# Whole rows for twelve of the sixteen second-layer weight tiles, on one Trainium2 core

## The chip, the core and the metric

The program runs on one NeuronCore of a Trainium2 chip. Its engines are TensorE (PE: matrix products, with weight loads listed apart as PEld), VectorE (DVE), ScalarE (ACT), GpSimd (POOL) and SyncE (SP). SyncE computes nothing here: its queue issues all DMA transfers, in order, to sixteen DMA engines. The metric is the device time of one execution in microseconds, as the median of several runs.

## The reference

A Nystrom attention (8 batches of 576 tokens, 8 heads of 64) feeds a gated MLP (512 to 1536 to 512), and this a soft mixture of 8 experts with 4 slots each. The last part, which the change is in, is this:

```python
logits = x @ phi                                  # 4608 tokens x 32 slots
d = softmax(logits, over tokens); c = softmax(logits, over slots)
slot_input = (d.T @ x).reshape(8, 4, 512)
for e in range(8):
    h = np.maximum(slot_input[e] @ w1[e], 0.0)    # w1[e]: 512 x 1024
    slot_out[e] = h @ w2[e]                       # w2[e]: 1024 x 512
return c @ slot_out.reshape(32, 512)              # 4608 x 512, float32
```

## The kernel before

The batches go through attention, gated MLP and slot logits in a long pipeline that fills the first 577 us. What follows is the tail. The slot inputs are summed up and multiplied through (lines 1159 to 1202), and the 32 slots pass the experts' two layers. The weights of these, 16.8 MB each, come from memory in tiles of 1 MB, `ffn_load(t, ...)` (line 1029): tiles 0 to 15 are `w1`, in rows of 512 columns, and tiles 16 to 31 are `w2`.

A tile of `w2` holds 256 rows of the hidden dimension (two blocks `c` of 128) and 256 of the 512 output columns, for four experts; two DMAs load it, one for each block. Tiles 16 to 23 belong to the left column half (`dh = 0`), tiles 24 to 31 to the right one. There are 22 buffers (`ffn_tags`, line 1049). `pump(n)` (line 1152) issues the loads up to tile n as buffers come free: tile t takes the buffer of tile t - 22.

Both layers multiply four experts side by side: a product of 128 rows of weights writes the 32 partitions of its expert in one PSUM tile. The first layer (line 1226) runs in two halves `nh` of the hidden dimension, each closed by a ReLU into `hF` (line 1235), four transposes (line 1238) and two copies into `FT`, from which the second layer takes its left operands. Hidden blocks 0 to 3 come from the first half.

The second layer (line 1273) runs once for each column half: 64 products of 256 columns add up in PSUM, lines 1288 and 1289 make `SR` out of the sum (high and low parts, for products in the fast float format), and `outputs(dh, SR)` (line 1250) multiplies the softmax weights of all 4608 tokens with it. That takes 36 products of 128 tokens by 256 columns; two share a PSUM tile, which ScalarE or VectorE in turn copies to an output buffer `ob`, and after 2, 4, 8, 16, 24, 32 and 36 blocks of 128 tokens (`GROUPS`) SyncE is told to write the group out, in rows of 1 KB.

The softmax weights `c` of a batch have to be turned before they can be left operands. `c_split(b)` (line 1206) does this for one batch: it splits the weights into parts (lines 1212 to 1215, on ScalarE, VectorE and GpSimd), turns them with five transposes on TensorE (lines 1219 and 1223), and copies the result out of PSUM (lines 1221 and 1224). All eight batches use the same working area, so that one split follows the other. In the text a *split* is one such call. They are written after the products of each of the tiles 16 to 23, so all before the first outputs.

What is written down is not the order in which an engine runs: in this part a planner orders each engine's instructions by the written order and by its own estimate of when each is ready. SyncE's queue and the engines then run that order as it stands.

Of the kernel before, what the change touches and what calls it, by code (L numbers as in the profile page):

```python
# [8 lines left out]
F32 = mybir.dt.float32  # L9
F32R = mybir.dt.float32r  # L10
AF = mybir.ActivationFunctionType
ALU = mybir.AluOpType
# [6 lines left out]
B, H, S, D = 8, 8, 576, 64  # L19
# [36 lines left out]
def nystrom_softmoe_kernel(  # L56
# [15 lines left out]
    pe, act, dve, pool, sp = nc.tensor, nc.scalar, nc.vector, nc.gpsimd, nc.sync  # L72
# [21 lines left out]
    psp = ctx.enter_context(tc.tile_pool(name="psp", bufs=1, space=PSUM))  # L94
# [9 lines left out]
    hi_sign, lo_mask = cst[:, 416:417], cst[:, 417:418]  # L104
# [15 lines left out]
    def big(tag, name):  # L120
        return bigp.tile([128, 2048], F32, tag=tag, name=name)
# [4 lines left out]
    def part(i, k):  # L126
        return HB[i][:, 2048 * k:2048 * k + 2048]
# [853 lines left out]

    TANH = [{(3, 1), (4, 0), (4, 1)}, {(1, 1), (2, 0), (2, 1)}]
    GROUPS = [2, 2, 4, 8, 8, 8, 4]


    pool.memset(one, 1.0)
# [6 lines left out]
    for x in S_["loads"]:  # L993
        k, n = x[0], x[1:]
# [31 lines left out]
    ffn_t = {}  # L1026

    def ffn_load(t, *bufs):
        if t < 16:
            nh, g, c = t // 8, (t // 4) % 2, t % 4  # L1030
            n = 4 // len(bufs)
            bt = []
            for i, buf in enumerate(bufs):
                src = w1[4 * g + n * i:4 * g + n * i + n, 128 * c:128 * c + 128, 512 * nh:512 * nh + 512]
                x = buf.rearrange("p (e f) -> p e f", e=n)
                sp.dma_start(x, src.rearrange("e p f -> p e f"))
                bt += [x[:, e, :] for e in range(n)]
        else:
            buf, = bufs
            dh, g, r = (t - 16) // 8, (t // 4) % 2, t % 4  # L1040
            bt = buf.rearrange("p (c e d) -> p c e d", c=2, e=4)
            for c in range(2):
                f0 = 256 * r + 128 * c
                sp.dma_start(bt[:, c], w2[4 * g:4 * g + 4, f0:f0 + 128, 256 * dh:256 * dh + 256].rearrange("e p d -> p e d"))
        ffn_t[t] = bt

    last = nb - 1
# [1 line left out]
    ffn_tags = ([f"fw{i}" for i in range(NW)] + ["00", "01", "02", "w3", "w4", "w5"] + [f"fx{i}" for i in range(NX)]  # L1049
                + ["12", "11", "w0", "w1", "w2"])  # L1050
# [4 lines left out]
    def wbuf(tag, name):  # L1055
        if tag[:2] in ("fw", "fx"):
            return (fwp if tag[1] == "w" else fxp)[0].tile([128, 2048], F32, tag=tag, name=name)
        return big(tag, name) if tag[0] == "w" else part(int(tag[0]), int(tag[1]))

    def ffn_prefetch(t):  # L1060
        ffn_load(t, wbuf(ffn_tags[t % len(ffn_tags)], f"ffn{t}"))
# [37 lines left out]
    for b in range(nb):  # L1099
        if b == 1:  # L1100
            middle = n_ins()
        for j in range(NJ):
            p = prev
# [48 lines left out]
    def pump(n):  # L1152
        while nxt[0] < min(n, 32):
            ffn_prefetch(nxt[0])
            nxt[0] += 1

    NT = len(ffn_tags)
    pump(NT - 3)
    m = psp.tile([128, 512], F32, tag="x", name="m_s", bufs=3)
# [8 lines left out]
    hF, SH = misc[:, 0:512], misc[:, 512:768].bitcast(F32R)  # L1168
# [11 lines left out]
    FT = part(1, 0).rearrange("p (g i x) -> p g i x", g=2, i=8)  # L1180
    pool.memset(FT, 0.0)
    m = psp.tile([128, 512], F32, tag="x", name="m_si", bufs=3)
# [6 lines left out]
    m = psp.tile([128, 512], F32, tag="x", name="m_sit", bufs=3)  # L1189
# [16 lines left out]
    def c_split(b):  # L1206

        if b % 2 == 0:
            cT[b // 2] = wbuf(ffn_tags[11 + b // 2], f"cT{b // 2}").bitcast(F32R)[:, 0:2 * S]
        c3 = misc[:, 768:1408].bitcast(F32R).rearrange("p (k j a x) -> p k j a x", k=5, j=4, a=4)  # L1210
        ch = CN[:, b].rearrange("p k (j x) -> p k j x", j=4)
        act.copy(c3[:, :, :, 0, :], ch)
        dve.tensor_copy(c3[:, :, :, 1, :], ch)
        dve.tensor_tensor(out=c3[:, :, :, 2, :], in0=ch, in1=c3[:, :, :, 0, :], op=ALU.subtract)
        pool.memset(c3[:, :, :, 3, :].bitcast(F32), 0.0)
        m = psp.tile([128, 512], F32, tag="x", name="m_ct", bufs=3)
        c3f = c3.bitcast(F32).rearrange("p k j a x -> p k (j a x)")
        for k in range(4):
            pe.transpose(m[:, 128 * k:128 * k + 128], c3f[:, k, :], ident)  # L1219
        o = cT[b // 2][:, S * (b % 2):S * (b % 2) + S]  # L1220
        act.copy(o[:, 0:512], m)
        m = psp.tile([128, 512], F32, tag="l", name="m_ct2")
        pe.transpose(m[:, 0:64], c3f[0:64, 4, :], ident[0:64, 0:64])  # L1223
        dve.tensor_copy(o[:, 512:576], m[:, 0:64])

    for nh in range(2):
        m = psp.tile([128, 512], F32, tag="pg", name="m_f1", bufs=2)
        for g in range(2):
            for c in range(4):
                t = 8 * nh + 4 * g + c  # L1230
                for e in range(4):
                    pe.matmul(m[32 * e:32 * e + 32, :], ZP[c][:, 4 * g + e, :], ffn_t[t][e],  # L1232
                              start=(g, c) == (0, 0), stop=(g, c) == (1, 3))
                pump(t + 1 + NT)
        act.activation(hF, m, AF.Relu)
        m = psp.tile([128, 512], F32, tag="x", name="m_ft", bufs=3)
# [10 lines left out]
    free = ffn_tags[15:21] + ffn_tags[10:11] + ffn_tags[0:2]  # L1247
    nob = [0]

    def outputs(dh, SR):  # L1250
        k0, nk = 0, nb * S // 128
        for n in GROUPS:
            n = min(n, nk - k0)
            if n <= 0:
                break
            ob = wbuf(free[nob[0] % len(free)], f"ob{nob[0]}").rearrange("p (k d) -> p k d", k=8)
            nob[0] += 1
            for k in range(k0, k0 + n, 2):
                w = min(2, k0 + n - k)
                m = psp.tile([128, 512], F32, tag=("pg", "pv")[k // 2 % 2], name="m_o", bufs=2)  # L1260
                for i in range(w):
                    t, o = divmod(128 * (k + i), 2 * S)
                    pe.matmul(m[:, 256 * i:256 * i + 256], cT[t][:, o:o + 128], SR, start=i == 0, stop=i == w - 1)  # L1263
                o = ob[:, k - k0:k - k0 + w, :].rearrange("p k d -> p (k d)")
                if k // 2 % 2:
                    act.copy(o, m[:, 0:256 * w])  # L1266
                else:
                    dve.tensor_copy(o, m[:, 0:256 * w])  # L1268
            sp.dma_start(out[128 * k0:128 * (k0 + n), 256 * dh:256 * dh + 256].rearrange("(k p) d -> p k d", p=128),
                         ob[:, 0:n, :])  # L1270
            k0 += n

    for dh in range(2):
        m = psp.tile([128, 512], F32, tag="pg", name="m_f2", bufs=2)
        for g in range(2):
            for r in range(4):
                t = 16 + 8 * dh + 4 * g + r
                for c in range(2):
                    for e in range(4):
                        pe.matmul(m[32 * e:32 * e + 32, 0:256], FT[:, g, 2 * r + c, 32 * e:32 * e + 32],  # L1280
                                  ffn_t[t][:, c, e, :], start=(g, r, c) == (0, 0, 0), stop=(g, r, c) == (1, 3, 1))
                pump(t + 1 + NT)
                if dh == 0 and 4 * g + r < nb:
                    c_split(4 * g + r)
        if dh == 0:
            SR2 = wbuf(ffn_tags[21], "SR")
        SR = SR2[:, 256 * dh:256 * dh + 256].bitcast(F32R)
        act.activation(SH, m[:, 0:256], AF.Copy, scale=hi_sign)  # L1288
        dve.scalar_tensor_tensor(out=SR, in0=m[:, 0:256], scalar=lo_mask, in1=SH, op0=ALU.mult, op1=ALU.add)  # L1289
        outputs(dh, SR)  # L1290


# [54 lines left out]
```

## Time and profile before

| | us |
|---|---|
| median of 3 runs | 662.58 (660.92 to 663.43) |
| the profiled execution | 661.27 |
| its span, first to last instruction | 659.2 |

The profile shows one execution. Times in it count from the span's start. An instruction group has its line, the engine, the tile written and the tiles read, and the busy time; TensorE's instructions overlap, so what one costs is read from the chain, where each piece counts only what it added. A DMA share near 1 means that all sixteen DMA engines are busy; it can exceed 1 by a little. A DMA that SyncE issues stands in its timeline with the time that issuing it took.

### The profile page before, as it was taken

How to read it: one execution, taken by the hardware profiler on the slowest of the kernel's cores; microseconds unless marked ns; L12 is line 12 of the kernel's file. 1: busy time of each engine (PE TensorE's matmuls, PEld its weight loads, DVE VectorE, ACT ScalarE, POOL GpSimd, SP SyncE). 2: the span in 40 equal slices, each digit the busy share in tenths (PEclk: the TensorE clock that was granted, in tenths of full speed). 3: DMA queues.
4: the chain of work that ended last, by engine and by line, in shares of the span. 5: the costliest groups of instructions: out<-in, count | busy, mean ns of one | idle time of the engine just before them, and what ended most of it. 6: DMA issues, size and time to landing. Idle time of an engine off the chain costs nothing. (4 is left out here: it accounts for less than half of the span.)

```text
span 659.2 us, 18308 instructions
## 1 busy us (share of the span) xinstructions
PE 620.1 (94%) x7591; PEld 464.7 (70%) x7591; DVE 471.8 (72%) x1154; ACT 300.1 (46%) x764; POOL 72.6 (11%) x81
## 2 busy tenths in 40 slices
PE   5699899999999999999999999999999999989991
PEld 2576677777777877777777877787778877743561
DVE  4999989889578687859785978597857555550441
ACT  2566985465338223823382338233822442320441
POOL 0410012013011101210120013001300000010000
PEclk9699999999999999999999999999999999999996
DMA  7889774453022222222222231222130596599999
GB/s 283 280 300 340 297 269 146 123 180 95 2 74 85 76 73 77 85 75 73 91 69 75 73 108 55 73 73 74 24 122 2 146 387 223 205 327 348 348 371 330
DMA packets 63298, 106.47 MB, mean 162 GB/s; under 512 B 4976, under 2 KB 33008, under 8 KB 61680
## 3 DMA queue, kind: packets, MB, share of 16 engines
q1 hardware_dynamic: 63216, 105.32, 47.6%
q8 instruction: 59, 0.97, 0.6%
q14 instruction: 23, 0.19, 0.1%
HBM read 91.24 MB, written 12.58 MB: 158 GB/s over the span
## 5 line engine op out<-in xcount | busy, mean ns | idle before, releaser
L313 ACT ACTIVATE u<-pg 128x288 f32<-128x288 f32 x174 | 71.9, 413 | 161.3 <-PE pg L946 152.7
L975 DVE TENSOR_TENSOR hT<-u,pv 128x288 f32<-128x288 f32 x174 | 78.0, 449 | 44.2 <-PE pv L946 37.9
L946 PE MATMUL pg<-EH,GH 128*128 128x288 f32 x384 | 93.9, 325 | 2.3 <-ACT u L313 1.4
L780 DVE TENSOR_TENSOR GL<-g,GH 128x512 fp32r<-128x512 f32 (+1 forms) x122 | 65.5, 568 | 33.6 <-ACT GH L766 33.6
L946 PE MATMUL pg<-EH,GL 128*128 128x288 f32 x384 | 86.1, 299 | 1.4 <-DVE GL L780 1.0
L946 PE MATMUL pv<-EH,GH 128*128 128x288 f32 x384 | 84.3, 299 | 0.3 <-ACT GH L766 0.3
L946 PE MATMUL pg<-EL,GH 128*128 128x288 f32 x384 | 82.7, 296 | 0.0
L946 PE MATMUL pv<-EL,GH 128*128 128x288 f32 x384 | 82.3, 295 | 0.0
L946 PE MATMUL pv<-EH,GL 128*128 128x288 f32 x384 | 82.1, 294 | 0.0
L766 ACT CAST GH<-g 128x512 fp32r<-128x512 f32 (+1 forms) x122 | 54.2, 496 | 55.1 <-PE g L749 55.0
L946 PEld LDWEIGHTS pg<-EH,GH 128*128 128x128 f32 x384 | 59.6, 189 | 25.2 <-issue 18.0
L800 DVE STREAM_TRANSPOSE HB<-hT 128x576 f32<-128x576 f32 x96 | 74.3, 774 | 1.8
L946 PEld LDWEIGHTS pg<-EH,GL 128*128 128x128 f32 x384 | 62.3, 188 | 5.1 <-DVE GL L780 4.2
L946 PEld LDWEIGHTS pv<-EH,GH 128*128 128x128 f32 x384 | 61.6, 188 | 2.4 <-issue 1.8
L946 PEld LDWEIGHTS pg<-EL,GH 128*128 128x128 f32 x384 | 61.6, 188 | 0.7 <-issue 0.7
L946 PEld LDWEIGHTS pv<-EL,GH 128*128 128x128 f32 x384 | 61.5, 188 | 0.7 <-issue 0.7
L946 PEld LDWEIGHTS pv<-EH,GL 128*128 128x128 f32 x384 | 61.6, 188 | 0.5 <-issue 0.5
L749 PE MATMUL g<-w,WB 64*32 64x512 f32 (+1 forms) x976 | 56.5, 510 | 0.4 <-ACT WB L536 0.4
L795 PE MATMUL l<-hT,P_sb 128*32 128x160 f32 (+1 forms) x768 | 44.7, 298 | 1.5 <-DVE hT L975 1.1
L795 PEld LDWEIGHTS l<-hT,P_sb 128*32 128x32 f32 x768 | 15.1, 108 | 40.4 <-DVE hT L975 15.8
L914 PE MATMUL m_d<-HB,HB 32*32 32x384 f32 x864 | 35.2, 491 | 0.0
L914 PE MATMUL m_d<-HB,DN 32*32 32x384 f32 x288 | 35.1, 491 | 0.0
(248 smaller groups left out, 940.4 us busy)
## 6 DMA issues: line engine op xcount, KB each, us to landing
k<-in_kT_dram SPq DMA_DIRECT2D x52, 288.0 KB, 3.8
ffn<-in_w_dram SPq DMA_DIRECT2D x13, 1024.0 KB, 8.8
ffn<-in_w_dram SPq DMA_DIRECT2D x24, 512.0 KB, 8.8
HB<-in_w_cat_dram SPq DMA_DIRECT2D x8, 1024.0 KB, 8.4
v<-in_v_dram SPq DMA_DIRECT2D x8, 1024.0 KB, 5.9
q<-in_qT_dram SPq DMA_DIRECT2D x28, 288.0 KB, 3.0
HB<-in_w_out_dram SPq DMA_DIRECT2D x12, 512.0 KB, 6.2
wr<-in_w_cat_dram SPq DMA_DIRECT2D x4, 1024.0 KB, 9.1
```

What stands on the lines that cost most here:

```text
L313: i = act.activation(*a, **kw)
L749: pe.matmul(gs[r][32 * hp:32 * hp + 32, 0:256 * n].rearrange("p (u f) -> p u f", u=n), WB[b % 2][64 * r:64 * r + 64, hp, :], w[64 * r:64 * ...
L766: act.copy(H_, g)
L780: dve.tensor_tensor(out=GL, in0=g, in1=GH, op=ALU.subtract)
L795: pe.matmul(L[32 * c:32 * c + 32, 0:32 * k], P_sb[:, j, :], main[:, 0:k, c, :], start=j == 0, stop=j == NJ - 1)
L800: dve.transpose(HB[b % 2][:, S * j:S * j + S].rearrange("p (t r) -> p t r", r=32), hT[:, 0:S].rearrange("p (t r) -> p t r", r=32))
L914: pe.matmul(ms[a][32 * g:32 * g + 32, 0:384].rearrange("p (j f) -> p j f", j=NJ), d_of(a, g, k), hb[32 * a:32 * a + 32, :, 4 * k + g, :], ...
L946: pe.matmul(ps[:, 0:HALF], G_t[b, j, q, sel_][h], e[:, q, ts_], start=n == 0, stop=n == 5)
L975: dve.tensor_tensor(out=o, in0=u, in1=pv[:, 0:HALF], op=ALU.mult)
```

## The change

Tiles 16 to 27 of `w2` become whole: a tile holds one block of 128 hidden rows and all 512 columns of four experts, and one DMA loads it. The last four hidden blocks of the second group of experts stay in column halves, as tiles 28 and 29 (left) and 30 and 31 (right). The twelve whole tiles are multiplied first, in products of 512 columns, into one PSUM tile that ScalarE copies to `hF`. Then for each column half the two remaining tiles are multiplied, VectorE adds the copied sum, and `SR` and the outputs follow as before. Splits 0 to 3 are written after the first four whole tiles; splits 4 to 7 now stand in `outputs`, each ahead of the first group of blocks that needs it (4 and 5 ahead of the fifth group, 6 and 7 ahead of the sixth). The PSUM tiles of the second layer move from the tag `pg` to the tag `x`.

```diff
+    WHOLE = 12
...
+        elif t < 16 + WHOLE:
+            buf, = bufs
+            g, fc = divmod(t - 16, 8)
+            bt = buf.rearrange("p (e d) -> p e d", e=4)
+            sp.dma_start(bt, w2[4 * g:4 * g + 4, 128 * fc:128 * fc + 128, :].rearrange("e p d -> p e d"))
         else:
             buf, = bufs
-            dh, g, r = (t - 16) // 8, (t // 4) % 2, t % 4
+            dh, r = divmod(t - 16 - WHOLE, (16 - WHOLE) // 2)
             bt = buf.rearrange("p (c e d) -> p c e d", c=2, e=4)
             for c in range(2):
-                f0 = 256 * r + 128 * c
-                sp.dma_start(bt[:, c], w2[4 * g:4 * g + 4, f0:f0 + 128, 256 * dh:256 * dh + 256].rearrange("e p d -> p e d"))
+                f0 = 128 * (WHOLE - 8 + 2 * r + c)
+                sp.dma_start(bt[:, c], w2[4:8, f0:f0 + 128, 256 * dh:256 * dh + 256].rearrange("e p d -> p e d"))
...
+    split = set()
     def outputs(dh, SR):
...
+            for b in range((128 * (k0 + n) - 1) // S + 1):
+                if b not in split:
+                    c_split(b)
+                    split.add(b)
             ob = wbuf(free[nob[0] % len(free)], f"ob{nob[0]}").rearrange("p (k d) -> p k d", k=8)
...
+    m2 = psp.tile([128, 512], F32, tag="x", name="m_f2", bufs=3)
+    SR2 = wbuf(ffn_tags[21], "SR")
+    for i in range(WHOLE):
+        g, fc = divmod(i, 8)
+        for e in range(4):
+            pe.matmul(m2[32 * e:32 * e + 32, :], FT[:, g, fc, 32 * e:32 * e + 32], ffn_t[16 + i][:, e, :],
+                      start=i == 0, stop=i == WHOLE - 1)
+        pump(16 + i + 1 + NT)
+        if i < 4:
+            c_split(i)
+            split.add(i)
+    act.copy(hF, m2)
     for dh in range(2):
-        m = psp.tile([128, 512], F32, tag="pg", name="m_f2", bufs=2)
-        for g in range(2):
-            for r in range(4):
-                t = 16 + 8 * dh + 4 * g + r
-                for c in range(2):
-                    for e in range(4):
-                        pe.matmul(m[32 * e:32 * e + 32, 0:256], FT[:, g, 2 * r + c, 32 * e:32 * e + 32],
-                                  ffn_t[t][:, c, e, :], start=(g, r, c) == (0, 0, 0), stop=(g, r, c) == (1, 3, 1))
-                pump(t + 1 + NT)
-                if dh == 0 and 4 * g + r < nb:
-                    c_split(4 * g + r)
...
+        m3 = psp.tile([128, 512], F32, tag="x", name="m_f2", bufs=3)
+        cols = slice(256 * dh, 256 * dh + 256)
+        for r in range((16 - WHOLE) // 2):
+            t = 16 + WHOLE + (16 - WHOLE) // 2 * dh + r
+            for c in range(2):
+                fc = WHOLE - 8 + 2 * r + c
+                for e in range(4):
+                    pe.matmul(m3[32 * e:32 * e + 32, 0:256], FT[:, 1, fc, 32 * e:32 * e + 32], ffn_t[t][:, c, e, :],
+                              start=(r, c) == (0, 0), stop=fc == 7)
+        SR = SR2[:, cols].bitcast(F32R)
+        R_ = hF[:, cols]
+        dve.tensor_tensor(out=R_, in0=R_, in1=m3[:, 0:256], op=ALU.add)
+        act.activation(SH, R_, AF.Copy, scale=hi_sign)
+        dve.scalar_tensor_tensor(out=SR, in0=R_, scalar=lo_mask, in1=SH, op0=ALU.mult, op1=ALU.add)
         outputs(dh, SR)
```

## Rows read from the trace of the kernel before

**Rows 1.** The page, its second part: DMA share in 40 slices of the span.

```profile
DMA  7889774453022222222222231222130596599999
```

**Rows 2.** Stretches: busy time of each engine, granted clock, DMA share, GB/s (last).

```profile
586.00:587.00 1.00, 0.99 (x7) 0.80 (x10) 1.00 (x3) 0.00 (x0) 1.00 (x2) 1.00 0.99 242
...
600.00:610.00 10.00, 10.00 (x90) 3.11 (x82) 0.65 (x2) 1.18 (x3) 0.00 (x0) 1.00 1.09 348
...
620.00:631.00 11.00, 10.48 (x86) 7.63 (x78) 7.63 (x19) 7.71 (x16) 0.69 (x3) 1.00 1.10 348
...
632.00:644.00 12.00, 10.72 (x143) 7.09 (x136) 4.26 (x7) 3.78 (x8) 0.00 (x0) 1.00 1.09 383
...
644.00:656.00 12.00, 1.57 (x10) 1.16 (x10) 2.15 (x4) 1.58 (x3) 0.00 (x0) 0.67 1.09 386
...
656.00:657.00 1.00, 0.00 (x0) 0.00 (x0) 0.00 (x0) 0.00 (x0) 0.00 (x0) 0.50 0.66 231
```

**Rows 3.** Timeline of SyncE's queue: start, us spent issuing, line, tiles, count.

```profile
517.91 9.65 SPq L1036 DMA_DIRECT2D ffn<-in_w_dram  x6
...
585.27 3.06 SPq L1044 DMA_DIRECT2D HB<-in_w_dram  x4
...
625.25 1.25 SPq L1044 DMA_DIRECT2D HB<-in_w_dram  x1
...
626.59 2.58 SPq L1269 DMA_DIRECT2D out_dram<-ob  x2
```

**Rows 4.** The chain that ended last: start, us, engine, tile, line, count.

```profile
602.68 6.36 PE m_f L1232 x57
...
609.04 0.22 PE m_f L1280
...
610.45 0.66 PE m_ft L1238 x4
...
611.10 0.56 PE m_f L1280 x6
...
618.10 0.59 PE m_ct L1219 x4
...
620.33 0.59 PE m_ct L1219 x4
...
621.12 1.46 PE m_f L1280 x22
...
623.64 0.52 PE m_o L1263 x2
...
624.19 0.70 DVE ob L1268
...
631.21 7.09 PE m_f L1280 x128
```

**Rows 5.** Stretches again, where first-layer weights are loaded.

```profile
519.00:520.00 1.00, 1.00 (x24) 0.43 (x26) 0.67 (x2) 0.08 (x1) 0.00 (x0) 1.00 0.83 143
...
536.00:544.00 8.00, 7.78 (x87) 5.99 (x88) 3.98 (x10) 2.78 (x9) 0.00 (x0) 1.00 1.05 386
```

**Rows 6.** DMA issues by tile: count, KB each, us from issue to landing.

```profile
HB<-DN SPq DMA_DIRECT2D x72, 20.0 KB, 1.8
```

**Rows 7.** Instruction groups by shape, 575 to 660: busy us, mean ns, idle before.

```profile
L1289 DVE SCALAR_TENSOR_TENSOR SR<-m_f,cst,Sacc 128x256 fp32r<-128x256 f32 x2 | 1.0, 483 | 7.9 <-ACT Sacc L1288 7.9
```

**Rows 8.** Timeline of ScalarE and VectorE, first half of the outputs.

```profile
626.41 0.33 ACT L1212 CAST Sacc<-CN 128x160 fp32r<-128x160 f32 x1
...
626.63 1.08 ACT L1266 COPY HB<-m_o 128x512 f32<-128x512 f32 x2
...
628.14 0.59 ACT L1221 CAST cT<-m_ct 128x512 fp32r<-128x512 f32 x1 [0.43 <-PE m_ct L1219]
...
628.66 2.35 ACT L1266 COPY ob<-m_o 128x512 f32<-128x512 f32 x4
...
631.25 0.69 DVE L1268 COPY HB<-m_o 128x512 f32<-128x512 f32 x1 [0.36 <-PE m_o L1263]
```

More of the change, by code (lines that the diff above doesn't have):

```diff
@@ L1271, in outputs @@
             k0 += n
-    for dh in range(2):
-        m = psp.tile([128, 512], F32, tag="pg", name="m_f2", bufs=2)
-        for g in range(2):
-            for r in range(4):
-                t = 16 + 8 * dh + 4 * g + r
-                for c in range(2):
-                    for e in range(4):
-                        pe.matmul(m[32 * e:32 * e + 32, 0:256], FT[:, g, 2 * r + c, 32 * e:32 * e + 32],
-                                  ffn_t[t][:, c, e, :], start=(g, r, c) == (0, 0, 0), stop=(g, r, c) == (1, 3, 1))
-                pump(t + 1 + NT)
-                if dh == 0 and 4 * g + r < nb:
-                    c_split(4 * g + r)
[L1285 to L1289, printed above, removed]
+    m2 = psp.tile([128, 512], F32, tag="x", name="m_f2", bufs=3)
[10 more added lines that the diff above has]
+    act.copy(hF, m2)
+    for dh in range(2):
+        m3 = psp.tile([128, 512], F32, tag="x", name="m_f2", bufs=3)
[12 more added lines that the diff above has]
+        dve.scalar_tensor_tensor(out=SR, in0=R_, scalar=lo_mask, in1=SH, op0=ALU.mult, op1=ALU.add)
         outputs(dh, SR)
```

## The prediction

> **What bounds the kernel now.** I read the page's DMA strip first, because the change is about transfers: through the last fifth of the span the sixteen DMA engines are full [rows 1]. The table by stretches, read next, says with what. From 600 to 631 the queue carries 348 GB/s at a share of 1.09 to 1.10 (three rows, alike); from 632 to 656 it carries 383 to 386 GB/s at the same share [rows 2]. The code tells the two apart: the loads of the second layer (16.8 MB, in rows of 256 columns, 1 KB) are all issued before the first output [rows 3], and everything goes through SyncE's one queue in order. So the slower stretch is the loads, the faster one the outputs. The outputs are 4608 x 512 x 4 B = 9.44 MB, 24.4 us at 386; the full rate stops at about 656.6 (231 GB/s in the microsecond from 656), so their bytes start at about 632.1, just where the rate steps up [rows 2].
>
> The list of SyncE's issues shows why they start then. The last load is issued at 625.25, the first output right behind it at 626.59 [rows 3], though its block left PSUM at 624.89 (624.19 plus 0.70 in the chain of waits) [rows 4]. The outputs wait for the loads ahead of them. TensorE holds nothing up: its second half of products ends at 638.30 (631.21 plus 7.09) [rows 4], while the first half's outputs, 12.2 us of bytes, move until about 644. The end is therefore: end of the loads, plus 24.4 us of outputs, plus 2.6 us to the span's end at 659.2. The run took 661.27 us, 2.07 beyond its span.
>
> **What the rows of 2 KB give.** Tiles 16 to 27 become one DMA each in rows of 512 columns. Rows of 2 KB are in the trace: from 536 to 544 only first-layer weights and the output projection move, both in 2 KB rows, at 386 GB/s [rows 5]. A tile is 1.049 MB: 3.01 us at 348, 2.72 at 386, so 0.296 us less each. Tile 16 does not count: the load behind it is issued only at 585.27, when a buffer comes free [rows 3], and the rate falls to 242 GB/s in the microsecond from 586 [rows 2]; a quicker tile 16 makes that dip longer. Eleven tiles x 0.296 = 3.3 us. The loads then end at 632.1 - 3.3 = 628.8. Bounds: 0, should w2's rows run as they do now, and 3.6 with all twelve. I take 3.3, since the 2 KB rows were read from a full queue, as these will be. The other four tiles keep 1 KB rows.
>
> The Trainium skill, page "DMA: Bandwidth & Descriptors", section Specifications, gives 512 B as the smallest transfer for line rate, by which 1 KB rows are at line rate already and this change would leave the loads' end at 632.1 (the third rival below). The 348 against 386 GB/s of this trace speak against that.
>
> **What the new order costs.** So far the first half of the outputs needed half the loads; now it needs tiles 16 to 29, all but two. The hand-over from loads to outputs, covered today, has to be worked out.
>
> *Loads.* Tile 29 is in at 628.8 - 2 x 3.01 = 622.8, plus 1 to 2 us until it is seen (20 KB take 1.8 us from issue to landing [rows 6]).
>
> *TensorE.* The first layer is untouched; its last transposes start at 610.45 and take 0.66 [rows 4]. The twelve tiles have 12 x 4 products of 512 columns, two instructions each (the 64 products of a half are 128 instructions [rows 4]): 96. Today 10 instructions of the second layer run before 610 (128 less the 118 in the six pieces from 611.10 to 621.12) [rows 4]; I give one tile, 8, the same place. A 512-column instruction costs 6.36/57 = 0.112 us, a 256-column one 7.09/128 = 0.055 [rows 4], so the wider product itself gains and costs nothing. 88 x 0.112 = 9.8. Four splits stand among them, 0.79 each (620.33 to 621.12 [rows 4]): 3.2. Products cut into by splits cost more: the six pieces take 7.73 us for 118 instructions, 1.2 over 118 x 0.055, so 0.24 for each of five splits; for four, 1.0. Then tiles 28 and 29, 32 x 0.055 = 1.8. Sum: 610.45 + 0.66 + 9.8 + 3.2 + 1.0 + 1.8 = 626.9. Tile 29's products begin near 626.0, so its load is hidden by 1 to 2 us. The copy of the 512 columns to SBUF lies beside the products of tiles 28 and 29 on an idle ScalarE.
>
> *To the first output.* From the last product to the first output product it takes 623.64 - 622.58 = 1.06 now, and the first block is out of PSUM 1.25 later [rows 4]. The added sum on VectorE is 128x256 out of PSUM, 0.48 by the one of that size [rows 7], with a hand-over 0.5. 626.9 + 1.06 + 0.5 + 1.25 = 629.7 for the first issue. From an issue into an empty queue to bytes: issued at 517.91 [rows 3], and in the microsecond before 520 it moved 143 KB [rows 5], 0.4 us at full rate, so 1.7 us. The outputs' bytes start at 631.4, against 632.1 now, and 2.6 us after the loads have ended. That gap is where the gain goes: 0.7 of 3.3 us is left.
>
> *Bounds of the hand-over.* The instructions do not run in the written order: eight splits are written ahead of the first half's end, but only five stand before 621.12 in the chain, and a piece of second-layer products runs inside the first layer at 609.04 [rows 4]. If the four later splits were drawn ahead of tile 29, TensorE would be 4 x (0.79 + 0.24) = 4.1 later and the end 3.4 later than now. At the other end, if the products were never late, the outputs would follow the loads directly: 3.3 earlier than now. I take the middle because the splits go one every 2.2 us (618.10 to 620.33 [rows 4]), so that four written early take 9 of the 16 us, and those written later stand behind tile 29.
>
> *Between output blocks.* Splits 4 to 7 now stand before the fifth and sixth output DMA. Each takes 0.33 and 0.59 of ScalarE [rows 8] and three short steps of VectorE, and the evictions behind them wait. Today the ends of three splits run there as well: with them, group 4 (blocks 8 to 15) was out of PSUM at 627.71, 4.07 after 623.64, and group 5 at 629.84, two of the four copies from 628.66, 6.2 after [rows 8]. The first issue comes 1.25 after; groups 1 to 3 are 8 blocks, 2.7 us of bytes, so group 4 is needed at 4.0 and is 0.1 late; group 5 is needed at 6.8 and, with about 1 us for one split more, is ready at 7.2. I put 0.3 us of empty queue for it (0 to 2). The second half's outputs have until 631.4 + 12.2 = 643.6. The first half's evictions end 8.3 after 623.64 now (631.94 [rows 8]), so about 9.3 after 628.5, at 637.8; then 1.8 for tiles 30 and 31, 1.6 for the sums, 1.25 and 1.7: 644.1 if none of these products ran in gaps, as some will. I take nothing, with up to 0.5.
>
> **Sum.** -0.7 + 0.3 = -0.4 us: the profiled run would go from 661.27 to 660.9. The median of the three runs is 662.58, 1.3 above the profiled one, so there I forecast 662.2.
>
> **The rivals.** (1) The hand-over closes: more products run ahead of the transposes, or the splits fall later, so that outputs are issued by about 627 and follow the loads without a gap. The full 3.3 us stays: 659.3. For it: TensorE pauses for the ReLU just before 610.45; against it: 2.6 us would have to be found, and the chain shows no other pause of TensorE up to 621 [rows 4]. (2) Slower: the splits run in the written order, each whole chain of 2.2 us before the next evictions. Then group 5 is out at 4.1 + 2 x 2.2 + 1.4 = 9.9 after the sums, against 6.8, and group 6 is late by 3.1 again: 6.2 us of empty queue in place of 0.3, 668.1. It decides once the queue idles over 4 us between the outputs. Against it: evictions and splits run mixed today [rows 8]. (3) The change doesn't do what it says: whole rows of w2 run at 348 as the half rows do. The loads end at 632.1, tile 29 is seen at 632.1 - 6.0 + 1.5 = 627.6, its products, sums and first block take 0.9 + 1.06 + 0.5 + 1.25, and with 1.7 the bytes start at 633.0: 0.9 later than now, with the 0.3 663.8. Against it: the 386 of the other 2 KB rows [rows 5].
>
> **Chances.** What a measurement of this kernel can tell from no change is about 0.5%, 3.3 us. Forecast 0.68, (1) 0.14, (2) 0.08, (3) 0.10. Rival 1 lies on the bound: half of it, and 0.03 of the forecast, count as faster: 0.10. Slower is rival 2 and 0.02 for the drawn-ahead splits: 0.10. Same: 0.80. The range goes from rival 1 (659.3) up to the splits drawn ahead (662.6 + 3.4 = 666.0), less a little as that is rare: 659.2 to 665.4.
>
> **What would show it.** Right: 386 GB/s for most of 590 to 620, loads done near 629, then two to three microseconds in which the DMA share falls, the first output's issue near 629.7, and the last bytes at 656. Wrong: no dip (rival 1), dips near the fifth and sixth output DMA (rival 2), 348 GB/s still (rival 3), or products of the second layer that wait for a load.

## The result, and the profile after

| | us |
|---|---|
| before, median of 6 runs | 661.86 (660.64 to 663.43) |
| after, median of 6 runs | 667.09 (666.71 to 667.35) |
| after / before | 1.0080, 95% interval 1.0069 to 1.0091 |
| the profiled execution of after | 666.95, span 665.2 |

The change makes the kernel slower, by 0.8% or 5.2 us, where I had forecast no difference (662.2, range up to 665.4). Spans give the same picture: 659.2 became 665.2.

As before, the DMA engines come first. This is the kernel after, from 600 to 665, in 40 slices of 1.6 us: the busy share in tenths, then GB/s.

```profile
DMA  9999999999999999951000899999999999999970
GB/s 387 384 389 387 379 387 386 389 387 383 362 343 347 352 350 352 350 166 37 0 0 0 294 347 343 333 332 338 347 343 339 332 384 386 388 369 345 348 243 6
```

The table by stretches of the same kernel (busy time of each engine, granted clock, DMA share, GB/s) puts numbers to its four parts:

```profile
590.00:616.00 26.00, 24.47 (x204) 8.40 (x200) 3.27 (x13) 4.54 (x13) 0.56 (x2) 1.00 1.05 387
616.00:628.00 12.00, 11.63 (x105) 3.92 (x97) 2.15 (x10) 3.01 (x7) 0.79 (x3) 1.00 1.09 351
...
628.00:636.00 8.00, 6.29 (x52) 3.68 (x53) 3.98 (x12) 3.73 (x8) 0.46 (x2) 1.00 0.08 26
...
636.00:652.00 16.00, 13.16 (x85) 9.93 (x84) 11.50 (x18) 9.38 (x17) 0.00 (x0) 0.89 1.03 340
...
652.00:656.00 4.00, 0.00 (x0) 0.00 (x0) 0.00 (x0) 0.00 (x0) 0.00 (x0) 0.81 1.09 386
656.00:660.00 4.00, 0.00 (x0) 0.00 (x0) 0.00 (x0) 0.00 (x0) 0.00 (x0) 0.50 1.06 364
```

The loads run at 387 GB/s where they ran at 348 [rows 2], as long as the rows are 2 KB; the last four tiles, in 1 KB rows, are back at 351. The loads' full rate ends near 628.2, and a thin rest of them runs on until 630 (127 and 57 GB/s in the microseconds from 628 and 629). Then comes what the kernel before did not have: from 628 to 636 there is next to nothing in the queue. The outputs follow at 340 GB/s, where they had 383 to 386 [rows 2]. They are back at 386 only from 652 to 658, and end at about 346.

Against before, the outputs' bytes start at 636.0 and not at 632.1 (+3.9), and take 26.8 us and not 24.5 (+2.3). Together +6.2, and the span is 6.0 longer.

SyncE's timeline after (start, us spent issuing, line, tiles, count) shows that the queue had nothing to send: the last load is issued at 622.96, the first output more than 12 us later, where 1.3 us lay between the two before [rows 3].

```profile
622.96 1.36 SPq L1050 DMA_DIRECT2D HB<-in_w_dram  x1
...
635.17 0.90 SPq L1281 DMA_DIRECT2D out_dram<-ob  x2
636.17 1.71 SPq L1281 DMA_DIRECT2D out_dram<-HB  x2
```

What made the first output late stands in TensorE's timeline after (start, us, line, operation, tiles, count; in brackets the idle time before it and what ended it). Line 1305 holds the products of the tiles in column halves, lines 1225 and 1229 the turnings of a split, line 1275 an output product:

```profile
624.98 1.06 PE L1290 MATMUL m_f<-ffn,HB 128*32 128x512 f32 x8
625.86 0.61 PE L1305 MATMUL m_f<-ffn,HB 128*32 128x256 f32 x8
626.41 0.66 PE L1225 MATMUL m_ct<-cst,Sacc 128*128 128x128 f32 x4
626.99 0.64 PE L1305 MATMUL m_f<-ffn,HB 128*32 128x256 f32 x8
628.41 0.63 PE L1225 MATMUL m_ct<-cst,Sacc 128*128 128x128 f32 x4 [0.78 <-DVE Sacc L1220]
628.97 0.27 PE L1229 MATMUL m_ct<-cst,Sacc 64*128 64x64 f32 x1
629.17 0.64 PE L1305 MATMUL m_f<-ffn,HB 128*32 128x256 f32 x8
630.39 0.63 PE L1225 MATMUL m_ct<-cst,Sacc 128*128 128x128 f32 x4 [0.58 <-DVE Sacc L1220]
630.95 0.27 PE L1229 MATMUL m_ct<-cst,Sacc 64*128 64x64 f32 x1
631.15 0.64 PE L1305 MATMUL m_f<-ffn,HB 128*32 128x256 f32 x8
632.37 0.63 PE L1225 MATMUL m_ct<-cst,Sacc 128*128 128x128 f32 x4 [0.58 <-DVE Sacc L1220]
...
633.91 0.39 PE L1275 MATMUL m_o<-SR,cT 128*128 128x256 f32 x1
```

Tiles 28 and 29 are four blocks of 8 instructions, and none of the four waits for its weights. But the planner put the four late splits, which are written inside `outputs`, in front of the second, third and fourth block and of `SR`. Each turning waits for the rest of its split on ScalarE and VectorE, and the products behind it on TensorE wait with it. The chain that ended last shows one such round (start, us, engine, tile, line, count):

```profile
628.41 0.63 PE m_ct L1225 x4
629.04 0.22 PE m_ct L1229
...
629.28 0.23 DVE cT L1230
...
629.56 0.34 ACT Sacc L1218
...
629.92 0.34 DVE Sacc L1220
...
630.39 0.63 PE m_ct L1225 x4
```

One round takes 1.98 us (628.41 to 630.39), of which the block of products fills 0.43. The splits share one working area, so the next one begins only when the last one's turnings are done.

### The profile page after: what moved, and what is told of

The parts are those of the page before. It is cut to its first block, busy times and chain, and to the rows that moved or that the text cites. A ratio compares the mean times of both kernels' runs of the same rounds, so it can differ in the third digit from the quotient of the medians.

```text
span 665.2 us, 18104 instructions
## 1 busy us (share of the span) xinstructions
PE 622.6 (94%) x7495; PEld 462.1 (69%) x7495; DVE 473.3 (71%) x1156; ACT 300.5 (45%) x765; POOL 72.6 (11%) x81
```

## The experiments

The first theory: the order of the late splits (4 to 7) costs the most, since it holds the first output back. Its rivals: moving the splits between the output blocks costs by itself, wherever they run; or the outputs' lower rate, which the order need not explain, costs the most. A second question was what lowers that rate. A third, whether the gain of the 2 KB rows can be kept at all. In the diffs `tc.issue_after(i)` lets what follows be issued only behind instruction `i`.

### The order of the late splits

**e1_held: the kernel after, late splits held behind the first half's sums.**

```diff
...
                 if b not in split:
-                    c_split(b)
+                    with tc.issue_after(sums[0]), tc.issue_after(sums[1]), tc.issue_after(sums[2]):
+                        c_split(b)
...
```

`sums` are the last product of the half on TensorE, `SH` on ScalarE and `SR` on VectorE.

> The changed kernel, with splits 4 to 7 tied on TensorE, ScalarE and VectorE behind the first half's last product and sums. Theory A (order): the changed kernel lost its time because the planner drew the four late splits between the products of tiles 28 and 29, each chain about 2 us; the first output product then moves from 633.9 back to about 628.5, the first output is issued near 629.8 and the time falls by 4 to 5 us, to 662 to 663. If in addition the outputs that meet an empty queue go on at 340 GB/s instead of 386, 664 to 665. Rival B (hand-over between blocks): the splits cost the same between the output blocks, and the time stays at 666 or more.

Measured: 663.35 us (662.43 to 664.02), ratio 1.0028 (1.0018 to 1.0039), between the 662 to 663 of the order alone and the 664 to 665 with the low rate. TensorE's timeline has tiles 28 and 29 in one piece now, and the first output product at 629.05:

```profile
625.08 2.31 PE L1306 MATMUL m_f<-ffn,HB 128*32 128x256 f32 x30
629.05 1.22 PE L1276 MATMUL m_o<-SR,cT 128*128 128x256 f32 x8 [1.67 <-DVE SR L1312]
```

That is 4.9 us earlier than after, and by the ratios (1.0080 to 1.0028) 3.4 us of the 5.2 come back. The order of the splits is the larger part of the loss. It isn't all: the outputs still run at the low rate, with a hole at 640 to 642 (stretches of e1_held):

```profile
632.00:640.00 8.00, 6.68 (x46) 4.70 (x45) 5.28 (x15) 5.22 (x12) 0.70 (x3) 1.00 1.03 347
640.00:642.00 2.00, 1.63 (x24) 0.67 (x23) 1.00 (x2) 0.85 (x2) 0.00 (x0) 1.00 0.52 173
642.00:648.00 6.00, 4.55 (x28) 3.75 (x29) 4.49 (x8) 4.01 (x8) 0.00 (x0) 1.00 1.05 344
650.00:653.00 3.00, 0.00 (x0) 0.00 (x0) 0.43 (x1) 0.00 (x0) 0.00 (x0) 0.94 1.09 387
```

The hole lies inside the first half. SyncE's timeline has its fifth output issued at 636.11 and its sixth only at 640.38:

```profile
636.11 0.37 SPq L1282 DMA_DIRECT2D out_dram<-ob  x1
...
640.38 0.37 SPq L1282 DMA_DIRECT2D out_dram<-ob  x1
```

In between, splits 6 and 7, which the sixth needs, are turned one after the other (635.65 and 637.61 on TensorE). At 173 in place of about 345 GB/s for 2 us, the hole costs 1.0 us. So the first rival, splits between the output blocks, has a part in what is left.

**e2_four: the kernel after without the late splits.** The output blocks of batches 4 to 7 are multiplied with the turned weights of batches 0 to 3.

```diff
...
-            for b in range((128 * (k0 + n) - 1) // S + 1):
-                if b not in split:
-                    c_split(b)
-                    split.add(b)
...
                     t, o = divmod(128 * (k + i), 2 * S)
+                    t = t % 2
...
```

> The changed kernel without splits 4 to 7 at all: the blocks of batches 4 to 7 take the turned weights of batches 0 to 3, so four splits of work are left out. It prices all that the late splits cost, wherever they stand. Theory A: first output product near 628.5, time 661 to 663, within 1 us of the kernel that holds them back. Rival B: within 1 us of the changed kernel, 666 to 667, since the wait for tile 29 and the longer products set the hand-over.

Measured: 661.16 us (660.61 to 661.73), ratio 1.0001 (0.9992 to 1.0011). With the late splits' work gone altogether, the first output product still comes at 629.45 in the chain, like e1_held's, and the kernel only draws level with before. Holding the splits back (e1_held) thus gets two thirds of what leaving them out gets; e1_held's hole would be more than half of the rest. And even without them the 3.3 us of the rows do not show up in the time; the outputs ran at 344 GB/s:

```profile
632.00:648.00 16.00, 12.44 (x82) 9.38 (x80) 11.19 (x18) 9.42 (x17) 0.00 (x0) 0.89 1.04 344
648.00:652.00 4.00, 0.00 (x0) 0.00 (x0) 0.00 (x0) 0.00 (x0) 0.00 (x0) 0.50 1.09 386
```

**e3_late: the kernel before, with only the splits moved.**

```diff
...
+            for b in range((128 * (k0 + n) - 1) // S + 1):
+                if b not in split:
+                    c_split(b)
+                    split.add(b)
...
-                if dh == 0 and 4 * g + r < nb:
+                if dh == 0 and 4 * g + r < 4:
                     c_split(4 * g + r)
+                    split.add(4 * g + r)
...
```

> The kernel before with one part of the change alone: splits 4 to 7 moved into the outputs; column halves and 1 KB rows stay. Theory A: the outputs still queue behind the loads until 632, so nothing moves: 661.4 to 662.4. Rival B (late splits empty the queue between output blocks): 3 us or more above the kernel before, 665 or more.

Measured: 661.8 us (660.63 to 663.01), ratio 1.0011 (0.9998 to 1.0024). The move by itself costs nothing that can be told from zero, so that rival falls for a queue with loads in front of the outputs: in the old tiling the first output waits for these, and the outputs run at 379 and 378 GB/s in 632 to 644 and 644 to 656. Where the outputs had little in front of them, in e1_held, the same move left the hole of 1.0 us. The place of the splits costs where no queue covers it.

### The rate of the outputs

Theory: the outputs run slowly because the queue had run empty in front of them, whatever the tiling. Rival: something that the new tiling brings (the splits between the blocks, the buffers) slows them.

**e7_empty: the kernel before, with all its second-layer products ahead of the first output product,** so that the loads end and the queue empties before the first output. Rows, tiles and output groups are those of before; the sums use the PSUM tag `x`, as in the kernel after.

```diff
...
+    i0 = getattr(i0, "ins", i0)
+    for dh in range(2):
+        m = ms[dh]
...
-        outputs(dh, SR)
+        with tc.issue_after(i0):
+            outputs(dh, SR)
```

> The kernel before (column halves, 1 KB rows) with all 128 products of the second layer written ahead of the first output product, so that the loads end at 632 as before but the first output is issued only near 635, into an empty queue, and then in quick succession. It disputes the rate of 340 GB/s that the outputs of the changed kernel had until 651. Theory S (outputs that start on an empty queue run slower): they go at about 340 for most of their 9.44 MB, end near 665, time 667 to 669. Rival T (it is the sparse issue of output DMAs that keeps the rate low): these outputs are issued fast, run at 383 to 386 and end near 662, time 665 to 666.5.

Measured: 670.07 us, two runs (670.05 and 670.10), ratio 1.0130 (1.0106 to 1.0154). That is 1 us above the theory's 667 to 669: the planner drew all eight splits ahead, the first output product came at 637.79, and the first output was issued at 638.98 and not near 635. Its stretches:

```profile
634.00:640.00 6.00, 5.93 (x87) 3.79 (x80) 1.74 (x3) 1.77 (x4) 0.00 (x0) 1.00 0.04 11
642.00:654.00 12.00, 9.10 (x47) 7.44 (x46) 8.90 (x14) 6.68 (x13) 0.00 (x0) 0.86 1.04 337
656.00:660.00 4.00, 0.00 (x0) 0.00 (x0) 0.00 (x0) 0.00 (x0) 0.00 (x0) 0.63 1.09 386
```

The same output rows, from the same tiling, run at 337 GB/s soon after the empty stretch, where they had 383 to 386 behind the loads [rows 2]; their first two microseconds, 640 to 642, still had 374. The new tiling is not needed for the low rate.

**e12_filler: the kernel after, with the queue kept busy.** Three more loads of 1 MB stand behind the last weight tile, into buffers that nobody reads, and the outputs get another buffer for one of these.

```diff
...
-    free = ffn_tags[15:21] + ffn_tags[10:11] + ffn_tags[0:2]
+    free = ffn_tags[15:21] + ffn_tags[0:3]
...
+    for i, tag in enumerate((ffn_tags[10], ffn_tags[3], ffn_tags[4])):
+        idle = wbuf(tag, f"idle{i}").rearrange("p (e d) -> p e d", e=4)
+        sp.dma_start(idle, w2[0:4, 128 * i:128 * i + 128, :].rearrange("e p d -> p e d"))
...
```

> The changed kernel plus three useless loads of 1 MB in 2 KB rows, issued behind the last weight tile into buffers that nobody reads, so that the queue carries bytes from 628 until about 636.4, when the first outputs come. Instruction order of all compute engines as in the changed kernel. Theory S (a queue that ran empty leaves the outputs at 340 GB/s for some 15 us): with the queue kept busy the outputs go at 383 to 386, end near 661 instead of 662.8, and the kernel gets 1.5 to 2 us faster although it moves 3 MB more: 665.0 to 665.8. Rival (the slow rate comes with the order and pace of these outputs): outputs stay at 340, and the bytes end at 663 to 664: 667 to 668.5.

Measured: 667.58 us (665.49 to 668.94, 4 runs), ratio 1.0084 (1.0058 to 1.0109): no faster than after, and 2 us above the theory's time, in the range of its rival. The rate did what the theory expected at first, 380 GB/s through the stretch in which after had 340, and fell again later:

```profile
628.00:644.00 16.00, 12.69 (x102) 7.86 (x103) 9.30 (x21) 8.04 (x16) 0.46 (x2) 1.00 1.07 380
644.00:646.00 2.00, 1.93 (x15) 1.64 (x14) 1.87 (x3) 1.39 (x3) 0.00 (x0) 1.00 1.07 371
646.00:652.00 6.00, 3.65 (x22) 2.70 (x21) 4.06 (x7) 3.73 (x7) 0.00 (x0) 1.00 1.05 350
```

The three loads delayed the outputs' first bytes by about 1 us, to near 637, and the outputs were slow again from 646 on. So it bears the theory out for the first 7 us of the outputs only: there was no empty stretch here at 644, and the rate sank all the same. An empty queue goes before the low rate in e7_empty, but it isn't needed for it, and what lowers the rate stays open (last section).

### Can the gain of the 2 KB rows be kept?

**e4_whole8: the kernel after with eight whole tiles** instead of twelve (`WHOLE = 8`).

> The changed kernel with WHOLE = 8: eight whole tiles, eight in column halves, so that the first outputs need tiles 16 to 27 and four loads (12 us) are still to come behind them. Seven tiles x 0.296 us of faster loads = 2.1 us, loads end near 630. Theory A (only the late hand-over loses time): outputs are issued near 629 and follow the loads with less than 1 us between, time 659.8 to 661. Rival B: products of 512 columns and split columns cost it by themselves, 663 or more.

Measured: 662.02 us (661.05 to 663.13), ratio 1.0013 (1.0000 to 1.0026), not the 659.8 to 661 expected. The first output product comes at 627.47, early enough for the outputs to follow the loads, at 378 GB/s in 630 to 634. Then the rate falls, to 342 in 636 to 644, although the queue did not run empty there: the sixth output, behind all the late splits, was issued at 637.89, with the fifth still on its way. Between the halves the queue thins (238 in 644 to 646).

**e8_left10, e9_left12, e11_left8, e10_left6: left column halves first.** Ten, twelve, eight and six whole tiles are loaded whole, but multiplied as before in 256-column products: all left halves, then `SR` from their sum alone, then the right halves while the first half's outputs go out. The late splits (three in e8 and e9, two in e10 and e11) are held as in e1_held.

```diff
+    def product(m, dh, i):
+        if i < WHOLE:
+            w = ffn_t[16 + i][:, :, 256 * dh:256 * dh + 256]
+        else:
+            w = ffn_t[16 + WHOLE + half * dh + (i - WHOLE) // 2][:, i % 2]
...
+    m = psp.tile([128, 512], F32, tag="x", name="m_f2", bufs=3)
+    for i in range(16):
+        mm = product(m, 0, i)
...
+    finish(m, 0, need)
+    need(15)
+    finish(m2[0], 1)
```

> Ten whole tiles in rows of 2 KB, but multiplied by column halves: the left half of the whole tiles first, then tiles 26 to 28, sums and outputs; the right halves of the same buffers after that. No added sum, five splits ahead of the sums, three tied behind them. Nine tiles x 0.296 us = 2.7 us of faster loads, first output issued near 625 as before, so the queue does not run empty at the hand-over. Theory A (a late first output is all that ate the gain): 658.8 to 660. Rival: the second half's first output, needed by 641.6 now, comes near 642 and the queue empties there, 660.5 to 662.

> The same with twelve whole tiles: eleven x 0.296 = 3.3 us of faster loads, ended near 628.8. The first half needs tile 29, in near 623 and seen near 624.5, so sums near 626.5, first output issued near 627.7, its bytes from 629.4. Theory A: a gap below 1 us, 658.6 to 660. If outputs that meet an empty queue run at 340 GB/s whatever its length, 661 to 662.

> The same with eight whole tiles: seven x 0.296 = 2.1 us of faster loads, the second half's first output needed by 640.4 and issued near 640.7. Theory A with S: on the edge; 659.3 to 660.3 if the queue holds, 661 to 662 with outputs at 340 GB/s after 642 if it empties.

> Six whole tiles, multiplied by column halves, left ones first; six splits ahead of the sums, two tied behind them, as the kernel before runs them. Five tiles x 0.296 = 1.5 us of faster loads. First output issued near 625 to 626, the second half's near 640.7, needed by 641.0: the queue never runs empty. Theory A with S: 386 GB/s to the end and 659.8 to 660.6, 1.0 to 1.5 us faster than before. Rival (the queue empties between the halves): 661 to 662.

| whole tiles | us | ratio (95%) | GB/s of the outputs' weakest stretch |
|---|---|---|---|
| 12 (e9_left12) | 662.79 | 1.0019 (1.0006 to 1.0033) | 150 in 642 to 644, 197 in 636 to 638 |
| 10 (e8_left10) | 660.87 | 0.9990 (0.9976 to 1.0003) | 116 in 643 to 645 |
| 8 (e11_left8) | 661.06 | 0.9986 (0.9974 to 0.9998) | 99 in 642 to 644 |
| 6 (e10_left6) | 660.37 | 0.9983 (0.9970 to 0.9996) | 244 in 640 to 642 |

Now the outputs follow the loads without a gap in all but e9_left12 (267 GB/s in 626 to 628), and in the other three they run at 377 to 384. The hole moves to the seam between the halves; e9_left12 has a second one, in 636 to 638, in front of its sixth output, as e1_held has. By their times e8_left10 and e11_left8 came out as the expectation has it for a queue that empties there, and e9_left12 above both of its ranges. e10_left6 came out within its theory's range, but not by its mechanism, since the queue thinned here too. In e10_left6 (stretches):

```profile
630.00:640.00 10.00, 8.89 (x137) 5.13 (x136) 1.59 (x4) 2.13 (x4) 0.00 (x0) 1.00 1.09 384
640.00:642.00 2.00, 1.93 (x14) 1.64 (x15) 1.64 (x3) 1.19 (x3) 0.00 (x0) 1.00 0.69 244
642.00:656.00 14.00, 4.04 (x24) 2.94 (x23) 4.30 (x7) 3.71 (x7) 0.00 (x0) 0.74 1.03 338
```

The first output of the second half is issued at 641.08, hardly changed from before (640.63 there). Before, the queue still held the first half's outputs until about 644; here they are out by 641. TensorE's second half has become what is late, and the lower rate behind the hole then takes its share: 14 us at 338 in place of 386 are 1.7 us.

**e13_mix10 and e14_mix8: the second half sooner.** From e8 and e11: the first six (four) right-half blocks are multiplied before the last left ones, the others in portions between the output groups.

```diff
+    PLAN = [6, 6, 7, 9, 10, 11, 13]
...
-                need(nob[0] - late)
+                need(PLAN[nob[0]])
...
+        if i == WHOLE:
+            need(5)
```

> Ten whole 2 KB tiles instead of the first twelve, multiplied by column halves: left halves first, the last of them mixed with six right-half blocks, the other right halves worked between the output groups; three of the eight splits stay behind the first half's last product. Theory (the late splits' chains and an output queue that runs empty are what the change costs): the queue of outputs never runs empty, neither at the hand-over nor between the halves, outputs at 380 to 386 GB/s from 630 us on, nine loads that are 0.296 us shorter each give 2.7 us: 658.6 to 659.5 us. Rival (the second half's outputs come late however its products are laid): a stretch of under 250 GB/s between the halves and about 340 GB/s after it, 660.5 to 662 us.

> The same with eight whole tiles, four right-half blocks early and two splits behind the first half's last product. Theory: seven shorter loads give 2.1 us and no stretch of the outputs runs under 250 GB/s: 659.2 to 660.0 us. Rival: the queue empties between the halves as it did with the right halves worked in one piece, 661 to 662 us.

Measured: e13_mix10 662.00 us (661.01 to 662.78), ratio 1.0006 (0.9993 to 1.0018), the rival's time, though not its place for the hole; e14_mix8 660.21 us (658.78 to 661.80), ratio 0.9977 (0.9962 to 0.9992), just above the theory's. Their stretches, e13_mix10 first:

```profile
628.00:638.00 10.00, 10.00 (x96) 6.15 (x89) 5.96 (x14) 5.22 (x11) 0.47 (x2) 1.00 1.02 345
638.00:640.00 2.00, 1.16 (x11) 0.54 (x10) 0.97 (x2) 1.52 (x3) 0.00 (x0) 1.00 0.20 67
```

```profile
630.00:642.00 12.00, 10.81 (x106) 6.95 (x98) 6.53 (x14) 6.16 (x13) 0.23 (x1) 1.00 1.08 378
642.00:646.00 4.00, 3.94 (x25) 2.98 (x23) 3.36 (x5) 3.45 (x8) 0.00 (x0) 1.00 0.94 321
646.00:656.00 10.00, 0.45 (x2) 0.24 (x2) 1.29 (x2) 0.39 (x1) 0.00 (x0) 0.64 1.04 348
```

In e13_mix10 the right-half blocks ahead of the first output push its issue to 627.82, so late that the queue thins where the loads end (282 GB/s in 628 to 629); the rate is mostly low from there on, and at 638 the queue empties, still in the first half: its sixth and seventh output were issued only from 638.78 on, behind splits 6 and 7 (633.88 and 636.01 on TensorE).

```profile
638.78 1.00 SPq L1286 DMA_DIRECT2D out_dram<-HB  x2
```

In e14_mix8 it runs thin (321) and never empty. It is the fastest by its ratio, as good as e10_left6 within their intervals. Both beat both kernels, before by only 0.2%. By the ratios e14_mix8 keeps 1.5 of the 2.1 us that its seven counted tiles are shorter by, and e10_left6 1.1 of the 1.5 us of its five.

## Why the prediction was wrong

**What held.** *The rows.* 387 GB/s against 348 for 2 KB rows of `w2`, with the loads' full rate over at 628.2 and the last of them in by 630 (forecast 628.8). The Trainium skill, page "DMA: Bandwidth & Descriptors", section Specifications, gives 512 B as the smallest transfer for line rate; by it the loads would have gained nothing, and the trace after speaks against it as that of before did, 351 for the 1 KB rows next to 387. *The products.* 512 columns at a time cost what two times 256 do, 0.116 us an instruction in the longest piece of the chain after, where the forecast had 0.112:

```profile
617.78 1.85 PE m_f L1290 x16
619.64 0.59 PE m_ct L1225 x4
...
620.43 4.42 PE m_f L1290 x38
```

*The loads of tiles 28 and 29* kept nobody waiting. *The gap as such*, loads done before the outputs are ready, was seen; its length was not.

**The step that failed** is "Bounds of the hand-over". It named the case, the four later splits drawn ahead of tile 29, and set it aside "because the splits go one every 2.2 us, so that four written early take 9 of the 16 us, and those written later stand behind tile 29". They did not stand there: nothing in a split depends on `SR`, and the planner placed all four before it. That five of eight ran ahead in the kernel before [rows 4] was a count of what fitted there, and no rule for where the others go. Forecast for the first output product: 628.5; measured 633.91.

**The bound itself was too small as well**: 4.1 us on TensorE, for 4 turnings of 0.79 and 0.24 for each cut. That priced what TensorE does for a split, not what it waits for. Among the twelve tiles, pieces of 16 instructions (1.85 us) cover a split's steps on the other engines; a block of 0.43 us does not, and a split costs its whole round of 1.98. The last product of tiles 28 and 29 ended at 631.79, 4.9 behind the 626.9 of the forecast. Of this 0.9 has another source: the twelve tiles ended at 626.0 and not at 625.1, since none of their 96 instructions ran before the first layer's transposes, where I had put 8. The other 4.0 are the rounds. Another 0.5 came after the products: on VectorE the added sum (at 632.14) and `SR`'s last step (at 633.38) each stood right behind a step of a late split (line 1220 at 631.90, line 1230 at 633.24). Rival 2 had the right price, 2.2 us for a chain with nothing beside it, but put it between the output blocks; there e3_late shows it hidden, and e1_held shows 1.0 us of it, in front of the sixth output.

Of these 5.4 us, 0.8 came back: from the first issue, 635.17, to the first bytes, about 636.0, I had put 1.7 us, and it took 0.8 to 0.9. So the bytes started 4.6 later than forecast.

**The second step that failed** was no step at all: the sum carried the outputs' 24.4 us at 386 over from before. After the queue had run empty they ran at 340 for 16 us, which is 16 x (1 - 340/386) = 1.9 us, and at 345 to 364 near the end. So they took 26.8 us, where the forecast had 24.4 and 0.3 for idle time between the blocks. The rate of a queue that is always full was taken for the rate of the transfer; e7_empty shows the same rows at 337 with the tiling of before. Why they slow down stays open.

**Would it have been right otherwise?** With the late splits behind the first half's sums, e1_held, the first output product came at 629.05, 0.5 from the forecast, and the time at 663.35 and not 662.2. What is left is the lower rate and the hole in front of the sixth output. Rival 1, the hand-over without a gap, is what the variants with left halves first do, and it does not bring 659.3 either: the first half's outputs are then out before the second half is ready.

## What to carry to other kernels

A bound on work that may be drawn ahead has to be priced as a whole round through all its engines, where nothing covers it, and a place in the written order is no evidence of a place in the run order unless a dependency makes it so. When a stretch of loads gets shorter, ask what the transfers behind it were waiting for: here the loads had hidden the splits, the first half's hand-over and the second half's products, and each became late in turn. Add up the time of transfers at the rate that they had in the same state of the queue, not at the best rate in the trace.

## What the runs showed of the hardware

The same transfers run at two rates, about 340 to 350 and about 386 GB/s. Rows of 1 KB that are read ran at 348 to 350 from 618 to 626 in all the kernels, a stretch with a full queue. Rows of 1 KB that are written ran at 377 to 386 behind the loads, and at 335 to 348 over 6 to 16 us behind an empty or thin stretch. Busy engines alone don't slow them: before wrote 387 in 640 to 642 with VectorE busy for 1.88 and ScalarE for 1.60 of the 2 us, and e1_held wrote 346 in 653 to 656 with every compute engine idle. Nor is it a matter of writing alone. In the loads of the whole tiles, with the same instructions in the kernel after and in e1_held, the rates from 590 to 600 were (after first):

```profile
590.00:600.00 10.00, 9.24 (x85) 3.41 (x81) 1.04 (x5) 0.98 (x5) 0.00 (x0) 1.00 1.05 388
```

```profile
590.00:600.00 10.00, 9.24 (x86) 3.37 (x82) 1.04 (x5) 0.98 (x5) 0.00 (x0) 1.00 1.02 346
```

Both come behind the thin stretch at 586 that the wait for a buffer leaves (274 and 289 GB/s there); one recovers at once, the other has 307 and 282 in 590 to 594 and 395 only from 596 on, and its loads end 1 to 2 us later.

What decides between the two stays open. For the writes a full queue goes with the high rate, but e12_filler and e4_whole8 lost it without an empty stretch. In six kernels (after, e1_held, e2_four, e4_whole8, e7_empty, e12_filler) the high rate came back between 647 and 656, for 4 to 7 us, and in the second half of the variants with left halves first it did not. It does not come back a fixed time after the queue was empty or thin: about 16 us in after (636 to 652), and 3 in e4_whole8 (645 to 648).

Counted in bytes from the first one, these fast stretches are nearly the same outputs each time, around the fourth of the second half. That one is written from the buffer `ffn_tags[16]`, and outputs from this buffer ran at the high rate in all the kernels (in e10_left6 up to the hole that cuts one short). In e9_left12 and e13_mix10, where it serves the fourth and the fifth output of the first half, those are the fast ones (384 to 386 in 632 to 635, 386 in 635.5 to 637.5), with slow ones around them. In before, outputs from all the buffers ran at 377 to 387. So the source buffer may have a part in the low rate; no run changes it by itself, and it is not shown.
